# One visit of small TensorE tiles per slot beside the first batch's MLP, in a fused attention and MLP kernel

## The chip, the cores and the metric

The kernel runs on one core of one Trainium2 chip. The metric is the device time of one execution in microseconds (us). The kernel before takes 1423.95 us, the median of 7 runs (1421.37 to 1427.73).

## What is computed

Attention with normed queries and keys, then an MLP on the attention's output, in float32 (the two weight matrices arrive as float64):

```python
q_n, k_n = rmsnorm(q, g_q), rmsnorm(k, g_k)          # q, k, v: batch 8, heads 12, seq 448, head 64
attn = softmax(q_n @ k_n.T / sqrt(64))
x = (attn @ v), heads side by side: (3584, 768)
h = x @ w_in                                          # w_in (768, 2048)
out = (h - tanh(h)) @ w_out                           # w_out (2048, 768)
```

## The kernel before, in words

**Steps and slots.** The attention is cut into 48 steps s = 0 to 47, one for each batch and pair of heads, six (NP) for a batch. The program is written as a hand-made order (manual schedule): each engine executes its queue in the order in which the Python code issues instructions. One *slot* s issues the attention of step s, and preparations for steps s+1 to s+4. Slots -3 to 5 are `first_slot` (L879): attention only, no MLP. Slots 6 to 11 are `early_slot` (L913): the attention of the second batch beside the MLP of the first. Slots 12 to 47 are `slot` (L941): the attention of a batch beside the MLP of the batch before it.

**The MLP as a stream.** `mlp()` (L847) is a generator that yields after each matmul. `run(ns)` (L858) takes matmuls from it until so many nanoseconds of TensorE time, by a fixed price of each matmul, are used up. `gap_ns(s)` (L870) is a twelfth of the half of the MLP that runs beside three slots. So a slot's share of the MLP is four gaps in all, and the calls of `run` say between which pieces of attention the MLP stands. For the first batch the slots 6 to 8 run beside `hidden(0)` (L690, x times w_in as 4 sets of 7 products, L669) and the slots 9 to 11 beside `project_first` (L807, L834, 96 matmuls of 448 columns).

**The attention of one step** has these parts on TensorE, all of them with tiles smaller than the array:
- `scores(s, c)` (L486): for the key chunk c = 0, 1, 2, one matmul per head of 448 columns (L499), and for the rest of the keys (c = KF = 3) four of 224 columns. Each head's scores go to one PSUM bank, and ScalarE turns the bank into probabilities with an exponential (L504).
- `totals(s, dn)` (L557): the sum of the probabilities by a product with ones (L572) into one bank `dn`, then a reciprocal on VectorE (L577) that reads the bank. For s up to 9 the product runs over all chunks (16 matmuls). From s = 10 on VectorE has added the chunks before (`add` L513, `add_last` L524), and 4 matmuls are left. From s = 13 on (FOLDED) the sum takes another way, and `totals` is not called.
- `last_values` (L531, L539, 8 matmuls) and `values` (L544, L551, 24 matmuls): probabilities times v, into two banks `av`.
- `divide` (L607): VectorE multiplies the `av` banks by the reciprocals (L613) into xT, the MLP's input. For the last three pairs of a batch GpSimd makes differences of xT (L628 to L631).

Not small: `turn` (L410), eight transposes on the whole array (L415, L419), copied out by ScalarE (L417, L423).

**Banks.** PSUM has eight banks: three `mm` for the MLP and five `sc` for the attention, each set handed out in turn (`bank_of`, L198). A matmul that gets a bank waits until its reader of five allocations ago is done.

**The weights.** Beside the first slots and the first batch's MLP the kernel also turns the float64 weights into float32, in 32 pieces (`weight`, L290): a transfer into one of three `w_raw` buffers (L265, L269), two ScalarE passes (L71, L72), three VectorE passes (L78, L79, L82), and one GpSimd pass (L90), after which the buffer is free for the transfer three pieces on. Sets of w_in get sums and differences on VectorE (L324) and are stored for later batches (`keep_weights`, L329, seven transfers L332). The MLP's products call `weight` by a list of due times (`due`, L637), and `project_first` calls it with every sixth matmul. All of these stand in the same queues as the attention's exponentials, reciprocals and divisions.

**Norms.** `squares` (L393, ScalarE L123, L124) then `norm` (L396: VectorE L133, L134, GpSimd's power L135) then `norm_q` (L401: VectorE L404) prepare step s+3.

Of the kernel before, what the change touches and what calls it, by code (L numbers as in the profile page):

```python
# [137 lines left out]
def bounded_path(tc, ctx, q, k, v, moe_w_in, moe_w_out, out, g_col, ident, ones, half_ones, neg_half, early):  # L138
# [22 lines left out]
    NP = H // 2  # L161
# [13 lines left out]
    KF, KR = S // P, S % P  # L175
# [32 lines left out]
    def load(s, names):  # L208
        b, hp = steps[s]
        for name in names:  # L210
            src = {"q": q, "k": k, "v": v}[name]
            if s == 0 and name != "v":
                t = early[name]
            else:
                shape = [CP, 2, NCH, D] if name == "q" else [P, NCH, 2, D] if name == "k" else [P, 2, NCH, D]
                t = nat.tile(shape, F32, name=f"{name}_nat", bufs=3 if name == "v" else 2)
                fetch(nc, name, t, src[b, 2 * hp : 2 * hp + 2], by_blocks(s))
            loaded[name, s] = t
# [174 lines left out]
    def squares(s):  # L393
        squares_of(nc, early["sq"], early["n"], loaded["q", s], loaded["k", s])
# [15 lines left out]
    def turn(s, tk, tq):  # L410

        rr, n = normed.pop(s), early["n"]
        kn = loaded.pop(("k", s))
        for c in range(NCH):
            nc.tensor.transpose(tk[:, c * P : (c + 1) * P], kn[:, c].rearrange("p h d -> p (h d)"), ident)  # L415
        kT = qkp.tile([P, S], F32, name="kT")
        nc.scalar.mul(kT, tk[:, :S], g_col)  # L417
        for c in range(NCH):
            nc.tensor.transpose(  # L419
                tq[:, c * CP : (c + 1) * CP], n[:, c].rearrange("p h d -> p (h d)"), ident[:CP, :CP]  # L420
            )
        qT = qkp.tile([P, S], F32, name="qT")
        nc.scalar.copy(out=qT, in_=tq[:, :S])  # L423
        turned[s] = rr, kT, qT
# [5 lines left out]
    def by_blocks(s):  # L430
        return has(s) and steps[s][0] >= FIRST
# [51 lines left out]
    def sc_bank():  # L483
        return bank_of("sc")

    def scores(s, c):  # L486

        rr, kT, qT = turned[s]
        halves, keys, n = (1, P, S) if c < KF else (2, KR, HS)
        name, bufs = ("p", 2) if c < 2 else ("p_full", 1) if c < KF else ("p_last", 2)  # L490
        if c == 1:
            p = probs[s, 1] = probs[s, 0]
        else:
            p = probs[s, c] = pp.tile([P, 2, 2 if c < 2 else 1, n], F32, name=name, bufs=bufs)
        tiles = [sc_bank() for _ in range(2)]
        for i in range(halves):
            for h in range(2):
                r = slice(h * D, (h + 1) * D)
                nc.tensor.matmul(  # L499
                    tiles[h][i * keys : (i + 1) * keys, :n], lhsT=kT[r, c * P : c * P + keys],  # L500
                    rhs=qT[r, i * n : (i + 1) * n], start=True, stop=True,
                )
        for h in range(2):
            nc.scalar.activation(  # L504
                p[:, h, c if c < 2 else 0, :], tiles[h][:, :n], AF.Exp,
                scale=1.0 if rr is None else rr[:, 0, 2 * c + h : 2 * c + h + 1],
            )

    def full(s):

        return probs[s, 0][:, :, 0], probs[s, 1][:, :, 1], probs[s, 2][:, :, 0]
# [19 lines left out]
    def last_values(s, av):  # L531

        v_nat, p = loaded["v", s], probs[s, KF]
        for n in range(2):
            keys = slice(n * KR, (n + 1) * KR)
            for m in range(2):
                for h in range(2):
                    r = (2 * m + h) * BL
                    nc.tensor.matmul(  # L539
                        av[n][r : r + BL, :HS], lhsT=v_nat[keys, h, KF, m * BL : (m + 1) * BL],  # L540
                        rhs=p[keys, h, 0], start=True, stop=False,
                    )

    def values(s, av):  # L544
        v_nat, p = loaded.pop(("v", s)), full(s)
        for n in range(2):
            for c in range(KF):
                for m in range(2):
                    for h in range(2):
                        r = (2 * m + h) * BL  # L550
                        nc.tensor.matmul(  # L551
                            av[n][r : r + BL, :HS], lhsT=v_nat[:, h, c, m * BL : (m + 1) * BL],
                            rhs=p[c][:, h, n * HS : (n + 1) * HS], start=False, stop=(c == KF - 1),
                        )
        return av

    def totals(s, dn):  # L557

        parts = [t[:, h, n * HS : (n + 1) * HS] for t in sums.get(s, ()) for n in range(2) for h in range(2)]
        parts = [(parts, [ones[:, :BL]] * 2)] if parts else []  # L560
        if not sums.pop(s):
            for p in full(s):
                parts.append(
                    ([p[:, h, n * HS : (n + 1) * HS] for n in range(2) for h in range(2)], [ones[:, :BL]] * 2)
                )
            last = probs[s, KF]
            parts.append(([last[:, h, 0] for _ in range(2) for h in range(2)], [half_ones[:, n] for n in range(2)]))
        for i, (moving, by) in enumerate(parts):
            for n in range(2):
                for h in range(2):  # L570
                    r = (2 * n + h) * BL
                    nc.tensor.matmul(  # L572
                        dn[r : r + BL, :HS], lhsT=by[n], rhs=moving[2 * n + h],
                        start=(i == 0), stop=(i == len(parts) - 1),
                    )
        rs = whole[s] = sp.tile([P, HS], F32, name="rs")
        nc.vector.reciprocal(rs, dn[:, :HS])  # L577
# [29 lines left out]
    def divide(s, av):  # L607
        b, hp = steps[s]
        rs = whole.pop(s)
        x = xT[b, hp] = xp.tile([P, S], F32, name="xT")  # L610
        for n in range(2):
            for m in range(2):
                nc.vector.tensor_tensor(  # L613
                    out=x[m * D : (m + 1) * D, n * HS : (n + 1) * HS],
                    in0=av[n][m * D : (m + 1) * D, :HS],
                    in1=rs[:, n * HS : (n + 1) * HS] if s >= FOLDED else rs[n * D : (n + 1) * D], op=ALU.mult,
                )
        for c in range(NCH):
            del probs[s, c]
        if hp < HC:  # L620
            return
        c = hp - HC
        if c == 0:
            tt[b] = tp.tile([P, 3, HC, HS], F32, name="tt", bufs=1)
        eng = nc.vector if b == 0 and c == HC - 1 else nc.gpsimd
        x11, x12, x21, x22 = (xT[b, r][:, n : n + HS] for r in (c, hp) for n in (0, HS))
        t1, t2, t4 = (tt[b][:, i, c] for i in range(3))
        eng.tensor_tensor(out=t1, in0=x12, in1=x11, op=ALU.subtract)  # L628
        eng.tensor_tensor(out=t2, in0=x22, in1=t1, op=ALU.subtract)  # L629
        eng.tensor_tensor(out=x12, in0=x22, in1=x12, op=ALU.subtract)  # L630
        eng.tensor_tensor(out=t4, in0=x21, in1=t2, op=ALU.subtract)  # L631
# [226 lines left out]
    def run(ns):  # L858

        spent[1] += ns  # L860
        while spent[0] + 1.0 < spent[1]:
            took = next(stream, None)
            if took is None:
                return
            spent[0] += took
# [4 lines left out]
    def gap_ns(s):  # L870

        if s < 2 * NP:
            return H_NS / 12 if s % NP < 3 else 4 * S / ENGINE_NS * CD * CF / 12
        return (H_NS + O_NS) / (4 * NP)

    def has(s):
        return 0 <= s < NS
# [32 lines left out]
        weight(EARLY * (s + 3) // (NP + 2))  # L910
        combine(2)

    def early_slot(s):  # L913
        gap = gap_ns(s)
        totals(s, sc_bank())
        if has(s + 1):
            scores(s + 1, 0)
            scores(s + 1, 1)
        if has(s + 2):
            load(s + 2, "v")  # L920
        run(gap)
        if has(s + 2):
            turn(s + 2, sc_bank(), sc_bank())
        if has(s + 3):
            squares(s + 3)
        if has(s + 4):
            load(s + 4, "qk")
        run(gap)
        if has(s + 1):
            scores(s + 1, KF)  # L930
        av = [sc_bank() for _ in range(2)]
        last_values(s, av)
        divide(s, values(s, av))
        if has(s + 1):
            scores(s + 1, 2)
        for work, n in ((add, 1), (add_last, 1), (norm, 3), (norm_q, 3)):
            run(gap / 2)
            if has(s + n):
                work(s + n)

    def slot(s):  # L941

        gap = gap_ns(s)
# [59 lines left out]
    for s in range(-3, NP):  # L1003
        first_slot(s)
    for s in range(NP, NS):
        (early_slot if s < 2 * NP else slot)(s)
    run(1e9)


# [343 lines left out]
```

## Time and profile before

| what | value |
|---|---|
| median of 7 runs | 1423.95 us |
| the profiled execution, time | 1428.92 us |
| its span in the profile | 1427.1 us |
| busy share of the span: TensorE (PE), its weight loads (PEld) | 97%, 82% |
| VectorE (DVE), ScalarE (ACT), GpSimd (POOL) | 65%, 33%, 37% |
| mean granted TensorE clock | 0.988 |
| start of slots 6, 7, 8 (first matmul of `totals`) | 86.94, 118.28, 148.50 us |
| start of slots 9, 10, 11 | 189.24, 226.53, 262.83 us |
| start of slot 12 | 294.78 us |

The profile is of one execution. "Busy" is the time in which an engine has an instruction under way; idle time stands with what ended it. The clock granted to TensorE is a share of full speed. A float32 matmul has two records, so 16 matmuls are "x32". The chain of waits is followed back from the last instruction. The table by stage gives, for each stretch of time, the busy time of each engine, the granted clock, the busy share of the DMA engines and the rate.

### The profile page before, as it was taken

The page shows a single profiled execution, that of the slowest core. Times are in us where ns is not written, and L with a number is a line of the kernel's source. Part 1 is how long each engine was busy: PE and PEld are TensorE (multiplying, and loading weights), DVE is VectorE, ACT ScalarE, POOL GpSimd, SP SyncE. Part 2 cuts the span into 40 slices and gives each one's busy share as a digit, 9 for nine tenths or more (in the row PEclk, how much of TensorE's full clock was granted, in tenths as well). Part 3 has the DMA queues.
Part 4 walks back from the last instruction along what each step waited for, and adds up shares of the span by engine and source line. Part 5 has one row for each costly group of instructions (what it writes and reads, how often), then busy time and mean ns, then how long its engine had stood idle before and what let it go on. Part 6 is the DMA issues. An engine that isn't in the chain of part 4 may idle for free.

```text
span 1427.1 us, 25566 instructions
## 1 busy us (share of the span) xinstructions
PE 1388.4 (97%) x9752; PEld 1165.4 (82%) x9752; DVE 928.3 (65%) x1571; ACT 467.2 (33%) x1070; POOL 524.2 (37%) x348
## 2 busy tenths in 40 slices
PE   6999899999999999999999999999999999999997
PEld 3568664478899799888989888987998888899997
DVE  3899878867655677557866577655775578632311
ACT  5765445223422333232332234223332333301100
POOL 4565545314521336214543145312362145401310
PEclk9999899999999999999999999999999999999999
DMA  8669788764565655665656666666556656365563
GB/s 185 157 187 240 234 245 211 216 193 154 158 172 153 169 165 179 170 169 157 182 151 180 169 159 176 174 157 169 158 175 174 172 159 179 123 184 169 193 191 89
DMA packets 355255, 249.72 MB, mean 175 GB/s; under 512 B 266484, under 2 KB 297396, under 8 KB 355124
## 3 DMA queue, kind: packets, MB, share of 16 engines
q1 hardware_dynamic: 355120, 248.00, 62.7%
q8 instruction: 79, 1.29, 0.4%
q14 instruction: 52, 0.43, 0.1%
q10 hardware_dynamic: 4, 0.00, 0.0%
HBM read 214.50 MB, written 33.42 MB: 174 GB/s over the span
## 4 chain that ended last, share of the span: by engine, by line
PE 87%; DVE 6%; DMA 2%; SPq 2%; ACT 2%; issue 1%; POOL 0%; ACTq 0%; DVEq 0%
PE mm L669 63%; PE sc L499 9%; PE sc L551 7%; PE mm L834 5%; PE sc L539 2%; DMA w_raw<-in_moe_w_out_dram 1%; DVE w_out L82 1%; SPq L265 1%; ACT sum_g L592 1%; DMA k_nat<-in_k_dram 1%; DMA gT<-in_moe_w_in_dram 0%; SPq L118 0%; DVE rs L577 0%; DVE rows L529 0%; DVE sum_T L586 0%
## 5 line engine op out<-in xcount | busy, mean ns | idle before, releaser
L669 PE MATMUL mm<-xT,w_f 128*128 128x224 f32 x1392 | 275.6, 354 | 0.0
L669 PEld LDWEIGHTS mm<-xT,w_f 128*128 128x128 f32 x1392 | 262.1, 190 | 9.1 <-issue 7.2
L669 PE MATMUL mm<-gT,w_f 128*128 128x224 f32 x1344 | 263.0, 354 | 0.0
L669 PEld LDWEIGHTS mm<-gT,w_f 128*128 128x128 f32 x1344 | 252.8, 190 | 11.4 <-issue 6.5
L457 POOL TENSOR_TENSOR rr_mine<-rr_mine,neg_half 128x28 f32<-128x28 f32 x30 | 145.1, 4837 | 251.8 <-DVE rr_mine L456 251.8
L669 PE MATMUL mm<-tt,w_f 128*128 128x224 f32 x1044 | 209.4, 354 | 5.4 <-DVE gT L706 5.4
L669 PEld LDWEIGHTS mm<-tt,w_f 128*128 128x128 f32 x1044 | 196.5, 190 | 11.4 <-DVE gT L706 7.5
L669 PE MATMUL mm<-tg,w_f 128*128 128x224 f32 x1008 | 197.7, 352 | 0.0
L706 POOL TENSOR_TENSOR gT<-s,th 128x448 f32<-128x448 f32 x96 | 115.8, 1216 | 212.7 <-ACT th L705 211.7
L669 PEld LDWEIGHTS mm<-tg,w_f 128*128 128x128 f32 x1008 | 190.6, 190 | 0.0
L499 PE MATMUL sc<-qT,kT 64*128 64x448 f32 (+1 forms) x960 | 168.3, 499 | 12.6 <-ACT p_last L504 9.3
L499 PEld LDWEIGHTS sc<-qT,kT 64*128 64x128 f32 (+1 forms) x960 | 70.3, 167 | 85.2 <-issue 59.7
L592 ACT COPY sum_g<-sum 32x14 f32<-32x14 f32 x280 | 56.3, 201 | 225.3 <-DVE sum L588 219.5
L613 DVE TENSOR_TENSOR xT<-sc,rs_T 64x224 f32<-64x224 f32 x140 | 54.4, 389 | 68.3 <-PE sc L551 66.3
L629 POOL TENSOR_TENSOR tt<-xT,tt 128x224 f32<-128x224 f32 x23 | 17.1, 744 | 221.9 <-DVE xT L613 221.8
L504 ACT ACTIVATE p<-sc 128x448 f32<-128x448 f32 x120 | 55.5, 548 | 97.8 <-PE sc L499 97.8
L135 POOL TENSOR_TENSOR rr<-rr,neg_half 112x8 f32<-112x8 f32 (+1 forms) x36 | 59.8, 1682 | 63.3 <-DVE rr L134 63.2
L705 ACT ACTIVATE th<-s 128x448 f32<-128x448 f32 x96 | 55.0, 578 | 85.4 <-DVE s L731 37.6
L551 PE MATMUL sc<-p,v_nat 128*32 128x224 f32 x1344 | 79.9, 355 | 0.0
L834 PE MATMUL mm<-gT,w_out 128*128 128x448 f32 x192 | 77.4, 561 | 0.0
L521 DVE TENSOR_TENSOR rows<-p 128x896 f32<-128x896 f32 x38 | 42.4, 1115 | 41.7 <-ACT p L504 41.7
L834 PEld LDWEIGHTS mm<-gT,w_out 128*128 128x128 f32 x192 | 37.0, 197 | 38.2 <-issue 36.7
(144 smaller groups left out, 1753.2 us busy)
## 6 DMA issues: line engine op xcount, KB each, us to landing
w_f<-w_in SPq DMA_DIRECT2D x196, 384.0 KB, 3.1
w_f<-w_out SPq DMA_DIRECT2D x147, 512.0 KB, 3.8
w_raw<-in_moe_w_out_dram SPq DMA_DIRECT2D x16, 768.0 KB, 5.1
out_dram<-th SPq DMA_DIRECT2D x192, 56.0 KB, 1.9
w_in<-w_out SPq DMA_DIRECT2D x21, 384.0 KB, 6.0
qk_nat<-in_q_dram SPq DMA_DIRECT2D x120, 56.0 KB, 2.3
qk_nat<-in_k_dram SPq DMA_DIRECT2D x120, 56.0 KB, 2.3
gT<-in_moe_w_in_dram SPq DMA_DIRECT2D x32, 192.0 KB, 3.9
```

Source lines behind the costliest of these rows:

```text
L135: nc.gpsimd.tensor_tensor(out=r, in0=r, in1=neg_half[:rows], op=ALU.pow)
L457: nc.gpsimd.tensor_tensor(out=mine, in0=mine, in1=neg_half[:, :1].to_broadcast([P, 2 * NJ]), op=ALU.pow)
L499: nc.tensor.matmul(tiles[h][i * keys : (i + 1) * keys, :n], lhsT=kT[r, c * P : c * P + keys], rhs=qT[r, i * n : (i + 1) * n], start=True, ...
L504: nc.scalar.activation(p[:, h, c if c < 2 else 0, :], tiles[h][:, :n], AF.Exp, scale=1.0 if rr is None else rr[:, 0, 2 * c + h : 2 * c + h ...
L521: nc.vector.tensor_tensor(out=t, in0=p[0], in1=p[1], op=ALU.add)
L551: nc.tensor.matmul(av[n][r : r + BL, :HS], lhsT=v_nat[:, h, c, m * BL : (m + 1) * BL], rhs=p[c][:, h, n * HS : (n + 1) * HS], start=False, ...
L592: nc.scalar.copy(out=acc[h * BL : (h + 1) * BL, g], in_=part[g * BL : (g + 1) * BL, h * NJ : (h + 1) * NJ])
L613: nc.vector.tensor_tensor(out=x[m * D : (m + 1) * D, n * HS : (n + 1) * HS], in0=av[n][m * D : (m + 1) * D, :HS], in1=rs[:, n * HS : (n + ...
L669: nc.tensor.matmul(bank[:, f * HS : (f + 1) * HS], lhsT=w[:, c * width + f, :], rhs=moving[p](c), start=(first and f == 0 and c == 0), sto ...
L705: nc.scalar.activation(th, h, AF.Tanh, bias=0.0, scale=1.0)
L706: eng.tensor_tensor(out=g[:, rows, cols], in0=h, in1=th, op=ALU.subtract)
L834: nc.tensor.matmul(bank[:, :S], lhsT=w_out_row(f, n // HC)[:, n % HC * P : (n % HC + 1) * P], rhs=g[:, f, :], start=(f == 0), stop=(f == C ...
```

## The change

`early_slot` is removed, and the slots 6 to 11 use `slot`:

```diff
-    def early_slot(s):
-        gap = gap_ns(s)
-        totals(s, sc_bank())
-        if has(s + 1):
-            scores(s + 1, 0)
-            scores(s + 1, 1)
-        if has(s + 2):
-            load(s + 2, "v")
-        run(gap)
-        if has(s + 2):
-            turn(s + 2, sc_bank(), sc_bank())
-        if has(s + 3):
-            squares(s + 3)
-        if has(s + 4):
-            load(s + 4, "qk")
-        run(gap)
-        if has(s + 1):
-            scores(s + 1, KF)
-        av = [sc_bank() for _ in range(2)]
-        last_values(s, av)
-        divide(s, values(s, av))
-        if has(s + 1):
-            scores(s + 1, 2)
-        for work, n in ((add, 1), (add_last, 1), (norm, 3), (norm_q, 3)):
-            run(gap / 2)
-            if has(s + n):
-                work(s + n)
...
     for s in range(NP, NS):
-        (early_slot if s < 2 * NP else slot)(s)
+        slot(s)
```

What `slot` issues for these six slots (the parts for later batches, which test `blocks` and `folded`, issue nothing here):

```python
    def slot(s):
        gap = gap_ns(s)
        scores(s + 1, KF)
        dn = sc_bank()
        av = [sc_bank() for _ in range(2)]
        last_values(s, av)
        totals(s, dn)
        divide(s, values(s, av))
        for c in range(KF):
            scores(s + 1, c)
        load(s + 2, "v")
        run(gap / 2)
        add(s + 1)
        run(gap / 2)
        turn(s + 2, sc_bank(), sc_bank())
        squares(s + 3)
        load(s + 4, "qk")
        run(gap / 2)
        add_last(s + 1)
        run(gap / 2)
        norm(s + 3)
        run(gap)
        norm_q(s + 3)
        run(gap)
```

So the two visits of small tiles, before at the slot's start and in its middle, become one at its start, with the sums' product between the last chunk's values and the other values. The same matmuls, exponentials, divisions and transfers are issued as before. `norm` stands after two gaps (before: three and a half), `norm_q` after three (before: four), `add` and `add_last` half a gap and one and a half gaps after the visit. Slots -3 to 5 and 12 to 47 are unchanged.

## Prediction, on record before the run

> **What bounds the kernel now.** I read the table by stage first, cut at the starts of slots. Its columns: stretch, length, busy time of TensorE, weight loads, VectorE, ScalarE, GpSimd, then granted clock, DMA share, GB/s. Slots 7 to 11 of before:
>
> ```profile
> 118.28:148.50 30.22, 30.22 (x238) 25.55 (x237) 28.06 (x38) 16.77 (x28) 19.16 (x13) 1.00 0.94 283
> 148.50:189.24 40.74, 34.81 (x237) 28.32 (x236) 33.31 (x39) 20.05 (x31) 18.60 (x10) 0.87 0.69 217
> 189.24:226.53 37.29, 34.98 (x189) 17.31 (x188) 32.23 (x35) 16.87 (x27) 23.19 (x15) 0.95 0.79 216
> 226.53:262.83 36.30, 34.65 (x165) 16.67 (x164) 32.40 (x46) 12.86 (x22) 19.45 (x13) 0.95 0.82 218
> 262.83:294.78 31.95, 31.95 (x165) 15.78 (x165) 22.82 (x37) 7.29 (x14) 8.13 (x7) 1.00 0.84 236
> ```
>
> Slots 7 and 11 are TensorE from end to end. Slot 8 has slot 7's matmuls and takes 10.5 us longer; slots 9 and 10 are 5.3 and 4.35 us longer than slot 11 (of the 5.3, 1.1 is the longer sums' product). VectorE is busy 28 to 33 us in each, so it has little slack. TensorE's waits between 86.94 and 294.78 us:
>
> ```profile
> PE sc L499 <- ACT p_last L504: 7.6, 2, 5.9
> PE sc L415 <- DVE rs L577: 2.3, 1, 2.3
> PE mm L669 <- DVE s L725: 0.3, 1, 0.3
> ```
>
> So 10.2 us of idle. ScalarE's rows by time at the longest wait show why: the exponential stands behind a weight pass that waits for its transfer.
>
> ```profile
> 171.82 0.91 ACT L71 ACTIVATE w_out<-w_raw 128x768 f32<-128x768 f32 x1 [5.11 <-DMA w_raw<-in_moe_w_out_dram]
> 172.63 0.90 ACT L72 ACTIVATE w_raw<-w_raw 128x768 int32<-128x768 uint32 x1
> 173.43 0.77 ACT L504 ACTIVATE p_last<-sc,rr 128x224 f32<-128x224 f32 x2
> ```
>
> Idle time costs twice. The table by stage after the waits of 5.9, 2.3 and 1.65 us shows the clock at half:
>
> ```profile
> 174.00:176.00 2.00, 2.00 (x3) 0.71 (x4) 1.60 (x5) 0.91 (x3) 1.63 (x1) 0.50 0.86 226
> ...
> 203.00:205.00 2.00, 2.00 (x4) 1.01 (x3) 1.97 (x3) 2.00 (x5) 1.17 (x1) 0.50 1.11 347
> ...
> 250.00:252.00 2.00, 2.00 (x4) 0.95 (x3) 1.91 (x4) 0.00 (x0) 1.92 (x3) 0.50 0.59 91
> ```
>
> The prices by clock are 0.13 of 40.74 (5.3 us) in slot 8, 0.05 of 37.29 (1.9) in slot 9, 0.05 of 36.30 (1.8) in slot 10.
>
> [...] Here 1.65 us of idle sufficed. [...]
>
> **What the change removes.** Nothing is computed less. Slot 12 of before already runs the new order; its visit by rows of TensorE:
>
> ```profile
> 294.78 0.61 PE L499 MATMUL sc<-qT,kT 64*64 64x224 f32 x8
> 295.32 0.61 PE L539 MATMUL sc<-p_last,v_nat 64*32 64x224 f32 x16
> 295.86 0.59 PE L572 MATMUL sc<-rows,ones 128*32 128x224 f32 x8
> ...
> 298.15 0.56 PE L551 MATMUL sc<-p_full,v_nat 128*32 128x224 f32 x8
> 298.64 2.79 PE L499 MATMUL sc<-qT,kT 64*128 64x448 f32 x12
> ```
>
> By the chain of waits this visit is 0.54 + 0.54 + 0.52 + 2.27 + 2.72 = 6.59 us; slot 11's two visits are 0.52 + 1.71 and 0.54 + 0.54 + 2.41 + 0.95, together 6.67. The first run of MLP matmuls after a visit is 0.18 us longer than one after the transposes (5.49 against 5.31 for 28). So one visit less saves 0.08 + 0.18 = 0.26 us a slot, 1.5 us in six. That is the sure part, and all of it if nothing else moves.
>
> **What it adds: a wait within the visit.** Before, the banks of `totals` and `values` were wanted again half a slot later. Now five banks serve one visit: `scores(s+1, 1)` takes the bank of `totals`, so it waits for the reciprocal, and the first `values` bank, and `scores(s+1, 2)` the second, so they wait for `divide`. Behind the waiting score stands all of TensorE. The cover is `values` and chunk 0's scores, 2.27 + 0.95 = 3.2 us; slot 12's visit shows no wait there. But beside the weights VectorE is late. In before the reciprocal followed the end of its product by:
>
> - slot 7: 5.4 us (125.35 against 119.94), slot 8: 3.3, slot 9: 8.7 (199.58 against 190.9), slot 10: 5.6 (232.71 against 227.1), slot 11: 2.1.
>
> With the reciprocal's 1.55 us and up to 1.64 us of divisions after it, a visit would wait between nothing and 7 us. What shortens the lags: `norm_q` (1.0 us alone, up to 3.05 us while GpSimd's power is late) leaves its place right ahead of the reciprocal, and GpSimd gets a gap instead of half a gap for the power. For each visit nothing and the old lag are the two ends.
>
> [...]
>
> **The walk, slot by slot**, with durations of before. An undisturbed slot is slot 7 less 0.26, 29.95 us (slots 6 to 8), or slot 11 less 0.15, 31.8 us (slots 10, 11). The last scores chunks begin 5.9 us after the start (slots 6 to 9) or 4.8.
>
> - *Slot 6* starts at 86.94. `last_values` waits for the exponentials that end at 88.26; `totals` ends at 90.25; the reciprocal, behind the weights' passes as before, ends at 94.96, the divisions at 96.6, the visit at 97.4. With four gaps and `turn` (22.2) slot 7 starts at 119.6: +1.4 us against before.
> - *Slot 7*: a wait of 0 to 3.0 us for VectorE; I take 2, nearer the old lag, since VectorE is full there. Slot 8 starts at 151.6: +3.1.
> - *Slot 8*: the reciprocal (153.45 to 155 before) is in time for 157.5. The wait of 5.9 us can't occur in its place: no exponential stands in mid-slot behind the weight pass, and the MLP's three banks let TensorE go on for a product or two (2.3 us each) while a tanh is late. Slot 9 starts at 181.5: -7.7.
> - *Slot 9*: the weights are late now. The exponentials of the visit stand behind the pass of the piece that was treated at 193.13 before. Its transfer waited for a chain that had itself stood still with TensorE (ScalarE's tanh waited for TensorE until 182.60), so it comes earlier, but seven stores fill the DMA engines until about 184 (400 GB/s). I put the exponentials at 191.3, between 186.5 (no wait) and 195.2 (as before). TensorE wants them at 186.5 and waits 4.8 us, pays some 2.5 us of clock, and ends the visit at 197. The 2.3 us wait of `turn` for the reciprocal, with its 1.9 us, goes: the reciprocal is over by then. With 25.2 us of MLP and `turn` slot 10 starts at 222.2: -4.3.
> - *Slot 10*: 31.8 plus 1 us of waiting for VectorE, in place of 36.30. Slot 11 starts at 255.0: -7.8.
> - *Slot 11*: 31.8 against 31.95. Slot 12 starts at 286.8: -8.0.
>
> The walk is too kind to VectorE: I took a weight piece's three passes at 2.06 us, while their means here, beside a busy GpSimd, are 852 + 895 + 1042 ns = 2.79 us. Four such passes lie on the chain that ends in slot 9's exponentials and slot 7's reciprocal: 3 us back. The forecast is **-5 us**.
>
> The profiled execution took 1428.92 us, 0.35% over the median of the runs, for a span of 1427.1. Made against it the sum gives 1423.9; a difference of -5 on the median of 1423.95 gives **1419.0 us**. About 0.2% (2.8 us) is what a measurement of this kernel can tell from no change.
>
> **Rivals.**
> 1. *VectorE's lag becomes the bound of the visits (slower).* Place: chunk 1's scores in slots 6 to 10. With the old lags the visits would wait 2.2, 3.9, 1.8, 7.2 and 4.1 us, 19 us, and five clock prices of 1.7 us, 8.5: 27.7 us. Against this go the 1.5 us saved and, of the old excess (9.5, 4.2 and 4.35), between 4.2 and 18. That gives +8 to +22; with half the lags gone +3. It decides once the reciprocal begins more than 1.7 us (3.2 less 1.55) after the product. For it: VectorE's busy 28 to 33 us. Against: the lags are work of VectorE that time spent waiting lets it finish. At its middle 1433 us; chance 0.28.
> 2. *The wait only moves (no change).* The pieces' chain (transfer, ScalarE, VectorE, GpSimd, three buffers) sets the pace, and slot 9's exponentials come at 195.2 as before. The visit then ends near 201, where before stands at 192.6 plus 4.4 for the visit still owed plus 4.2 for the wait of `turn`, 201.2. Slot 10's gain goes to a weight wait of its own. 1423; chance 0.17.
> 3. *No visit meets a late weight pass.* The excess of slots 8 to 10 goes but for a few us: -10 to -16, 1411; chance 0.05.
>
> That the program would not do what the diff says is excluded: built, TensorE's queue has the new order in all six slots.
>
> **How the numbers follow.** The forecast's own case (-3 to -10 us) has 0.50. Faster by over 0.2%: 0.50 + 0.05 = 0.55; within: 0.17; slower: 0.28. The range 1409 to 1433 takes in the forecast, no change, most of case 3 and half of rival 1; about 0.17 is left out.
>
> **What would show it.** Right: slot 8 near 30 us in place of 40.7; the largest wait at `scores` chunk 0 of slot 9, for an exponential (L504); no wait of L415 for L577; slots 6 and 7 1 to 3 us longer. Wrong: waits of L499 for L577 or L613 over 2 us in several slots (rival 1), or slot 9 starting early and ending late by the same amount (rival 2). From slot 12 on nothing should differ but the offset.

## The result, and the profile after

The changed kernel takes **1429.40 us** (median of 18 runs), the kernel before 1423.42 (46 runs): ratio 1.0040, 95% interval 1.0031 to 1.0049. It is slower by some 6 us; forecast was 1419.0, 5 us faster. A second set of its runs (e15 below) came out at 1.0023 (1.0008 to 1.0037): slower again, by some 3 us. The profiled execution of the changed kernel took 1430.26 us for a span of 1428.5.

The table by stage of the changed kernel, slots 6 to 11 (stretch, length, busy time of TensorE, weight loads, VectorE, ScalarE, GpSimd, then granted clock, DMA share, GB/s):

```profile
84.49:119.78 35.29, 33.68 (x239) 26.79 (x237) 32.44 (x46) 18.68 (x31) 16.12 (x10) 0.95 0.62 164
119.78:153.41 33.63, 32.48 (x238) 26.81 (x237) 26.96 (x38) 17.04 (x29) 18.26 (x12) 0.95 0.70 194
153.41:191.98 38.57, 32.78 (x238) 27.25 (x237) 35.75 (x43) 17.79 (x29) 22.20 (x12) 0.96 0.75 251
191.98:229.53 37.55, 34.38 (x190) 18.98 (x189) 29.49 (x36) 18.16 (x28) 22.68 (x15) 0.95 0.76 217
229.53:264.79 35.26, 34.39 (x166) 16.82 (x165) 31.75 (x41) 13.92 (x22) 20.13 (x12) 0.95 0.80 223
264.79:296.43 31.64, 31.64 (x166) 16.27 (x165) 22.17 (x37) 7.21 (x14) 6.44 (x5) 1.00 0.82 225
```

Against before (31.34, 30.22, 40.74, 37.29, 36.30, 31.95 us) the slots are longer by 3.95 and 3.41, shorter by 2.17, longer by 0.26, shorter by 1.04 and 0.31: together 211.94 against 207.84 us, +4.1. From slot 12 to the end nothing differs (1132.07 against 1132.32 us). The spans differ by 1.4 only, because slot 6 began at 86.94 us in before's profiled execution and at 84.49 in this one; in the runs e4, e5, e11 and e12 below, whose code is before's up to there, it began at 84.2 to 84.9. So the medians are the measure.

TensorE's waits in the changed kernel between 84.49 and 296.43 us (total, times, longest):

```profile
PE mm L669 <- DVE s L727: 4.3, 1, 4.3
PE sc L499 <- ACT p_last L504: 3.2, 1, 3.2
PE sc L499 <- DVE rs L577: 3.2, 3, 1.1
PE mm L669 <- DVE s L725: 1.5, 1, 1.5
...
```

This is 12.6 us where before had 10.2. The exponential's 5.9 us in slot 8 and the turn's 2.3 us in slot 9 are gone. In their place stand 4.3 and 1.5 us of MLP products in slot 8 that wait for VectorE's additions (L725, L727), three waits of scores for the reciprocal, and 3.2 us at the start of slot 9.

**The reciprocal in the visit.** VectorE by time in slot 7 of the changed kernel:

```profile
123.60 0.96 DVE L82 SCALAR_TENSOR_TENSOR w_f<-w_raw,w_f 128x768 int32<-128x768 int32 x1
124.47 0.95 DVE L324 TENSOR_TENSOR w_f<-w_f 128x768 f32<-128x768 f32 x1
125.34 1.55 DVE L577 RECIPROCAL rs<-sc 128x224 f32<-128x224 f32 x1
127.00 1.63 DVE L613 TENSOR_TENSOR xT<-sc,rs 64x224 f32<-64x224 f32 x4
```

TensorE in the same visit:

```profile
124.78 1.02 PE L499 MATMUL sc<-qT,kT 64*128 64x448 f32 x4
126.94 3.75 PE L499 MATMUL sc<-qT,kT 64*128 64x448 f32 x8 [1.15 <-DVE rs L577]
```

A weight piece's passes, of which the last (L82) is shown, and a sum (L324) stand ahead of the reciprocal. It ends at 126.89, and at 126.94 chunk 1's scores start, 1.15 us late.

**The wait that the list of waits doesn't have.** Those four score matmuls (x8: two records each) take 3.75 us. In slot 7 of before four of them ran so:

```profile
119.94 1.77 PE L499 MATMUL sc<-qT,kT 64*128 64x448 f32 x8
```

Part of the difference is the clock (below). The rest shows in the run e3, whose slot 7 is in the new form and ran at full clock:

```profile
124.55 1.02 PE L499 MATMUL sc<-qT,kT 64*128 64x448 f32 x4
126.71 2.76 PE L499 MATMUL sc<-qT,kT 64*128 64x448 f32 x8 [1.13 <-DVE rs L577]
```

The view of line L499 alone, in e3 between 124.5 and 129.8 us, counts weight loads with matmuls: idle time before them, and what ended it (us, times):

```profile
its engine sat idle before it (us, times) until:
  DVE rs L577: 3.0, 2
  DVE xT L613: 1.1, 2
  issue: 0.4, 1
```

Two heads' scores use half of the array's rows each (64) and run side by side: in chunk 0 their first matmuls start at 124.55 and 124.56. In chunk 1 the first head's bank comes from the reciprocal, the second's from the first half of the divisions. The heads start at 126.71 and 127.60 us, one after the other, and each takes some 0.9 us, the time in which both would run. Price: 2.76 less 1.77, **1.0 us** a visit. TensorE counts as busy in it, since the records overlap: in slot 7 of the changed kernel the first head's last record runs from 127.43 to 127.96, and the second head's first starts at 127.84. Slots 6 (e3: 2.79) and 10 (e13: 2.78) show the same, slot 8 a row of x12 with 3.41 us in place of slot 11's 2.76.

Before pays this price too, in its two waits for an exponential: the second head's scores of chunk 2 come after the wait, alone. Slot 10 of before, and slot 11, where nothing waits:

```profile
245.30 1.02 PE L499 MATMUL sc<-qT,kT 64*128 64x448 f32 x2
247.97 1.02 PE L499 MATMUL sc<-qT,kT 64*128 64x448 f32 x2 [1.65 <-ACT p_last L504]
...
281.60 1.02 PE L499 MATMUL sc<-qT,kT 64*128 64x448 f32 x4
```

After the wait the second head takes TensorE for 0.94 us more (the next matmul starts at 248.91). In slot 8 it takes 1.79 us, at half clock. So each of these two waits cost some 0.95 us beyond its length, the clock apart.

**The MLP in slot 8.** TensorE's two late products of the changed kernel:

```profile
178.71 2.54 PE L669 MATMUL mm<-xT,w_out 128*128 128x224 f32 x12 [1.48 <-DVE s L725]
185.55 4.04 PE L669 MATMUL mm<-xT,w_out 128*128 128x224 f32 x12 [4.31 <-DVE s L727]
```

VectorE meanwhile:

```profile
173.50 2.21 DVE L78 TENSOR_SCALAR w_out<-w_out 128x768 f32<-128x768 f32 x1
...
178.04 0.62 DVE L725 TENSOR_TENSOR s<-mm,s 128x448 f32<-128x448 f32 x1
178.57 1.94 DVE L78 TENSOR_SCALAR w_out<-w_out 128x768 f32<-128x768 f32 x1
180.54 0.56 DVE L79 TENSOR_SCALAR w_out<-w_out 128x768 int32<-128x768 int32 x1
181.14 0.96 DVE L82 SCALAR_TENSOR_TENSOR w_out<-w_raw,w_out 128x768 int32<-128x768 int32 x1
182.02 0.68 DVE L133 TENSOR_REDUCE rr<-n 112x8 f32<-112x512 f32 x1
182.73 1.45 DVE L134 TENSOR_SCALAR rr<-rr 112x8 f32<-112x8 f32 x1
184.10 0.67 DVE L133 TENSOR_REDUCE rr<-sq 128x8 f32<-128x512 f32 x1
...
184.88 0.62 DVE L727 TENSOR_TENSOR s<-mm,s 128x448 f32<-128x448 f32 x1
```

VectorE has no gap of more than 0.1 us here. Each addition that frees a bank of the MLP stands behind a weight piece, the second also behind `norm` (L133, L134), which now comes earlier. Before, VectorE caught up during TensorE's stand of 5.9 us in mid-slot, and then waited for TensorE itself:

```profile
179.09 0.62 DVE L727 TENSOR_TENSOR s<-mm,s 128x448 f32<-128x448 f32 x1 [3.39 <-PE mm L669]
```

**Slot 9.** ScalarE at the start of slot 9 of the changed kernel:

```profile
195.18 0.94 ACT L71 ACTIVATE w_out<-w_raw 128x768 f32<-128x768 f32 x1 [8.05 <-DMA w_raw<-in_moe_w_out_dram]
...
197.66 0.92 ACT L71 ACTIVATE w_out<-w_raw 128x768 f32<-128x768 f32 x1 [0.23 <-DMA w_raw<-in_moe_w_out_dram]
...
199.74 0.75 ACT L504 ACTIVATE p_last<-sc,rr 128x224 f32<-128x224 f32 x2
```

As foreseen, the visit's exponential stands behind weight passes that wait for a transfer; it came at 199.74, not at 191.3 (the wait was shorter than the walk's because slot 9 itself began late).

**The clock.** The table by stage of the changed kernel, cut into half microseconds, at the edges of what the clock lost:

```profile
94.00:94.50 0.50, 0.50 (x4) 0.26 (x4) 0.47 (x2) 0.16 (x1) 0.00 (x0) 0.75 1.04 215
97.50:98.00 0.50, 0.50 (x4) 0.47 (x3) 0.50 (x1) 0.50 (x1) 0.50 (x1) 0.83 0.00 0
128.00:128.50 0.50, 0.50 (x2) 0.13 (x2) 0.47 (x2) 0.50 (x1) 0.00 (x0) 0.89 0.58 147
```

A mean of 0.75 between 1.00 and 0.50 puts the fall in the middle of its half microsecond, at 94.25; 0.83 puts the return at 97.67: 3.4 us at half clock. The third row (0.89) puts the next fall at 128.39; the others, read in the same way, are at 186.41, 200.07 and 237.61. So there are five such stretches between slots 6 and 12, at most 1.7 us lost in each. Before has five as well (three of them in a row, from 171.07 to 181.31). What is lost I take as half of the time that TensorE is busy in them (before's second head above took 1.79 us at half clock, 0.94 at full): it is busy 16.92 us there in the changed kernel and 14.22 in before, where the wait of 5.9 us takes up part of the first. So the clock costs 8.5 us, before 7.1.

**The sum** in this pair of profiles: idle +2.4; the heads that no longer run side by side +3.65 (1.0 in slots 6, 7 and 10, 0.65 in slot 8) less before's 1.9; clock +1.4; one visit less in six slots -1.5. Together +4.05, where +4.1 was measured.

### The profile page after: what moved, and what is told of

Same layout as the page of the kernel before. It is cut to its first block, busy times and chain, and to the rows that moved or that the text cites. A ratio compares the mean times of both kernels' runs of the same rounds, so it can differ in the third digit from the quotient of the medians.

```text
span 1428.5 us, 25550 instructions
## 1 busy us (share of the span) xinstructions
PE 1388.1 (97%) x9752; PEld 1169.1 (82%) x9752; DVE 928.0 (65%) x1571; ACT 467.4 (33%) x1070; POOL 527.3 (37%) x348
## 3 DMA queue, kind: packets, MB, share of 16 engines
q8 instruction: 79, 1.29, 0.4%
## 4 chain that ended last, share of the span: by engine, by line
PE 85%; DVE 7%; DMA 3%; ACT 2%; issue 1%; SPq 1%; POOL 0%; ACTq 0%; DVEq 0%; POOLq 0%
PE mm L669 61%; PE sc L499 10%; PE sc L551 6%; PE mm L834 4%; PE sc L539 1%; DMA gT<-in_moe_w_in_dram 1%; DMA w_raw<-in_moe_w_out_dram 1%; DMA q_nat<-in_q_dram 1%; PE mm L551 1%; DVE rs L577 1%; DVE w_out L78 1%; ACT sum_g L592 1%; DVE w_out L79 1%; DVE rows L529 0%; DVE sum_T L586 0%
## 5 line engine op out<-in xcount | busy, mean ns | idle before, releaser
L669 PE MATMUL mm<-xT,w_f 128*128 128x224 f32 x1392 | 275.5, 353 | 0.0
L669 PEld LDWEIGHTS mm<-xT,w_f 128*128 128x128 f32 x1392 | 262.2, 190 | 8.5 <-issue 6.5
L669 PE MATMUL mm<-gT,w_f 128*128 128x224 f32 x1344 | 263.0, 354 | 0.0
L669 PEld LDWEIGHTS mm<-gT,w_f 128*128 128x128 f32 x1344 | 252.8, 190 | 11.4 <-issue 5.9
L669 PE MATMUL mm<-tt,w_f 128*128 128x224 f32 x1044 | 209.4, 354 | 5.4 <-DVE gT L706 5.4
L669 PEld LDWEIGHTS mm<-tt,w_f 128*128 128x128 f32 x1044 | 196.5, 190 | 11.4 <-DVE gT L706 7.5
L669 PE MATMUL mm<-tg,w_f 128*128 128x224 f32 x1008 | 197.7, 352 | 0.0
L669 PEld LDWEIGHTS mm<-tg,w_f 128*128 128x128 f32 x1008 | 190.6, 190 | 0.0
L499 PE MATMUL sc<-qT,kT 64*128 64x448 f32 (+1 forms) x960 | 172.6, 508 | 10.6 <-ACT p_last L504 4.5
L499 PEld LDWEIGHTS sc<-qT,kT 64*128 64x128 f32 (+1 forms) x960 | 74.2, 170 | 85.2 <-issue 56.3
L135 POOL TENSOR_TENSOR rr<-rr,neg_half 112x8 f32<-112x8 f32 (+1 forms) x36 | 60.2, 1693 | 70.8 <-DVE rr L134 68.6
```

Source lines behind the costliest of these rows:

```text
L135: nc.gpsimd.tensor_tensor(out=r, in0=r, in1=neg_half[:rows], op=ALU.pow)
L499: nc.tensor.matmul(tiles[h][i * keys : (i + 1) * keys, :n], lhsT=kT[r, c * P : c * P + keys], rhs=qT[r, i * n : (i + 1) * n], start=True, ...
L669: nc.tensor.matmul(bank[:, f * HS : (f + 1) * HS], lhsT=w[:, c * width + f, :], rhs=moving[p](c), start=(first and f == 0 and c == 0), sto ...
```

## The experiments

Theory A puts the loss into the visits, where TensorE waits for VectorE; its rival B puts it elsewhere, so that freeing the visit would not bring it back. "Idle" is the sum of TensorE's listed waits from slot 6 up to slot 12 in the run's profile, "half" the number of 3.41 us stretches at half clock there. Each run's ratio is to the runs of before made beside it (medians 1423.17 us for e1 to e4, 1424.98 for e5 to e8, 1424.18 for e9 to e12, 1423.67 for e13 to e15), so ratios compare better than medians.

| kernel | median us | ratio to before (95%) | idle us | half |
|---|---|---|---|---|
| before | 1423.42 | 1 | 10.2 | 5 |
| after | 1429.40 | 1.0040 (1.0031 to 1.0049) | 12.6 | 5 |
| e15 after again | 1427.95 | 1.0023 (1.0008 to 1.0037) | 12.4 | 5 |
| e1 scores later | 1422.23 | 0.9983 (0.9971 to 0.9996) | 8.9 | 4 |
| e2 scores twice | 1424.98 | 1.0007 (0.9994 to 1.0020) | 10.0 | 2 |
| e3 slots 6 to 8 | 1426.06 | 1.0013 (1.0001 to 1.0026) | 10.2 | 3 |
| e4 slots 9 to 11 | 1427.39 | 1.0024 (1.0013 to 1.0035) | 12.4 | 4 |
| e5 preparations only | 1419.55 | 0.9961 (0.9948 to 0.9975) | 6.8 | 2 |
| e6 visit only | 1442.04 | 1.0125 (1.0106 to 1.0143) | 19.9 | 7 |
| e7 before, light VectorE | 1415.44 | 0.9938 (0.9923 to 0.9953) | 7.8 | 2 |
| e8 after, light VectorE | 1419.67 | 0.9963 (0.9950 to 0.9977) | 9.2 | 3 |
| e9 before, no late loads | 1415.30 | 0.9931 (0.9912 to 0.9949) | 4.4 | 1 |
| e10 after, no late loads | 1423.99 | 0.9997 (0.9984 to 1.0009) | 8.1 | 2 |
| e11 later last scores | 1414.37 | 0.9929 (0.9911 to 0.9946) | 4.1 | 0 |
| e12 late norm, slot 6 | 1419.55 | 0.9967 (0.9953 to 0.9982) | 5.3 | 2 |
| e13 late norm, slot 8 | 1428.88 | 1.0030 (1.0015 to 1.0045) | 13.6 | 3 |
| e14 e1 with e13 | 1422.55 | 0.9989 (0.9977 to 1.0001) | 11.5 | 3 |

**e1: chunks 1 and 2 of the scores half a gap later, in slots 6 to 11** (against after)

```diff
+        split = s < 2 * NP
         if has(s + 1):
-            for c in range(KF):
+            for c in range(1 if split else KF):
                 scores(s + 1, c)
...
         run(gap / 2)
+        if split:
+            scores(s + 1, 1)
+            scores(s + 1, 2)
```

> The changed kernel, but in slots 6 to 11 the scores of chunks 1 and 2 stand half a gap later, after the first MLP matmuls, so that TensorE doesn't meet the reciprocal's bank in the visit. Theory A (the loss is TensorE's wait of 0.9 to 1.15 us for the reciprocal in slots 6, 7 and 10, and the clock that halves after it, 2 to 2.7 us more each): these waits go, 3 x 3.4 us less 6 x 0.26 us for the extra change between MLP and small tiles, so about 8 us faster than the changed kernel, ratio to before about 0.998 (0.996 to 1.000). Theory B (the loss lies in the moved norms, sums and loads, which stay where the change put them): no gain over the changed kernel, ratio 1.004 to 1.006.

TensorE's rows of the same scores in slot 7 of e1:

```profile
124.71 1.02 PE L499 MATMUL sc<-qT,kT 64*128 64x448 f32 x4
128.51 1.77 PE L499 MATMUL sc<-qT,kT 64*128 64x448 f32 x8
```

No wait for the reciprocal is left in any slot, every row of 8 takes 1.77 us, and slot 7 is 30.08 us long (the walk's undisturbed slot: 29.95). e1 is 0.6% faster than after, some 8 us: theory A's number came, and B's (no gain) did not. The matmuls and banks are those of after; only the time between freeing and use is longer.

**e2: chunk 0's scores multiplied twice in slots 6, 7 and 10** (against after)

```diff
...
-                scores(s + 1, c)
+                scores(s + 1, c, 2 if c == 0 and s in (6, 7, 10) else 1)
```

> The changed kernel, but in slots 6, 7 and 10 chunk 0's scores are multiplied twice into the same banks (the same values again): 0.95 us more work for TensorE just ahead of each of the three waits, nothing moved on any other engine. Theory A with the clock as the larger part of the price: the waits shrink from 1.1 to 0.2 us, the clock stays full, and each visit ends some 2 us earlier: 5 to 7 us faster than the changed kernel, ratio to before 0.999 to 1.001. Theory A without the clock (a wait costs its length): the added work takes the wait's place, no difference, 1.004. Theory B: the work is added on top, 1.005 or more.

With six matmuls more (x12) it is 0.3% faster than after. Its waits for the reciprocal were 1.99 us in slot 6 and 0.40 in slot 7, not 0.2 as expected, and no stretch at half clock followed either. The rows of 8 still take 2.79 and 2.76 us: the repeated matmuls fill the wait for the first bank, not the lag between the two heads' banks. So the lag is a cost by itself, apart from the wait and from the clock.

**e3 and e4: the change in slots 6 to 8 alone (e3), or in 9 to 11 alone (e4)**, both against before

```diff
-        (early_slot if s < 2 * NP else slot)(s)
+        (early_slot if NP + 3 <= s < 2 * NP else slot)(s)
```

> The change in slots 6 to 8 alone; slots 9 to 11 as in the kernel before. By the slots' lengths in the two profiles (after less before: +3.95, +3.4, -2.2 us for slots 6, 7, 8 and +0.3, -1.0, -0.3 for 9, 10, 11) it costs 5 us: ratio 1.0036, and more if slot 9 in its old form meets the late weights worse. If the loss were spread over all six slots (Theory B, what is moved is moved in each): about 1.002.

```diff
-        (early_slot if s < 2 * NP else slot)(s)
+        (early_slot if s < NP + 3 else slot)(s)
```

> The change in slots 9 to 11 alone; slots 6 to 8 as in the kernel before. By the same table it gains 1 us: ratio 0.9993; with the wait in slot 10 still there (3.4 us) and the old wait of the transposes in slot 9 gone (4.2 us). Theory B (spread over all six): about 1.002.

The halves add up: 0.13% and 0.24% to the whole's 0.40%. Both missed: e3 was to cost 0.36%, and I had not expected the second half to lose. What came is nearer theory B's 1.002 for each half: the loss is spread over both. In e4's profile slot 8 (old form) keeps the wait of 5.94 us, and slot 9's visit then waits 1.42 us for an exponential and 4.07 for the reciprocal; the turn's wait that goes was 2.3.

**e5: before's two visits, after's earlier `norm` and `norm_q`; e6: after's visit, before's later preparations** (both against before)

```diff
         run(gap)
+        norm(s + 3)
         if has(s + 1):
             scores(s + 1, KF)
...
-        for work, n in ((add, 1), (add_last, 1), (norm, 3), (norm_q, 3)):
-            run(gap / 2)
-            if has(s + n):
-                work(s + n)
+        run(gap / 2)
+        add(s + 1)
+        run(gap / 2)
+        add_last(s + 1)
+        norm_q(s + 3)
+        run(gap)
```

> The kernel before with its two visits per slot, but norms, norm_q and sums in slots 6 to 11 at the places where the change put them (norm after two gaps, norm_q after three, sums half a gap earlier in the order). Theory A (the loss is TensorE's wait for the reciprocal's bank in the one visit, so here nothing is lost): ratio to before 0.998 to 1.001. Theory B (the moved preparations cost the time): 1.003 or more.

```diff
-        totals(s, sc_bank())
-        if has(s + 1):
-            scores(s + 1, 0)
-            scores(s + 1, 1)
...
+        scores(s + 1, KF)
+        dn = sc_bank()
+        av = [sc_bank() for _ in range(2)]
+        last_values(s, av)
+        totals(s, dn)
+        divide(s, values(s, av))
+        for c in range(KF):
+            scores(s + 1, c)
...
```

> The other half alone: one visit per slot as in the change, but turn, norms, norm_q and sums in slots 6 to 11 at their places of the kernel before (norm after three and a half gaps, norm_q right at the slot's end, ahead of the reciprocal in VectorE's queue). Theory A: at least the change's loss, more where norm_q now stands between TensorE's product and the reciprocal: 1.004 to 1.010, with longer waits of L499 for L577. Theory B: about 1.000.

TensorE's waits in e5:

```profile
PE sc L499 <- ACT p_last L504: 4.9, 2, 4.1
PE mm L669 <- DVE s L735: 1.3, 1, 1.3
...
```

TensorE's waits in e6:

```profile
PE sc L499 <- DVE rs L577: 8.9, 4, 4.1
PE sc L499 <- ACT p_last L504: 7.9, 1, 7.9
...
```

This takes the change apart, but for one piece: the sums (`add`, `add_last`) stand in both runs where before has them, though e5's expectation has them moved. The one visit alone costs 1.25%, some 18 us: four waits for the reciprocal (1.92, 1.29, 4.14 and 1.53 us), one of 7.93 for the exponential, and seven stretches at half clock; that is more than I had expected. The earlier norms alone *gain* 0.39%, which I had not expected: with them no transposes wait for the reciprocal, and three of five stretches at half clock go. In the new order the earlier preparations (there with the sums) give back 0.85 of the 1.25%. I had treated the two as one edit.

**e7 and e8: VectorE lighter**, in before and in after (without L79, one of a weight piece's three passes)

```diff
-    nc.vector.tensor_scalar(
-        out=bits, in0=bits, scalar1=4, scalar2=1, op0=ALU.logical_shift_left, op1=ALU.logical_shift_right
-    )
```

> The kernel before without one of VectorE's three passes over the weights (L79, the shift of the bits, is left out, so the weights are wrong): 24 passes of 0.56 to 0.9 us less on VectorE beside slots 6 to 10. It is the yardstick of the next run. Both theories: some 3 to 10 us faster than before (0.993 to 0.998), by shorter waits in slots 8 to 10.

> The changed kernel without the same pass. Theory A (the reciprocal comes late because VectorE's queue is full of weight passes): the reciprocal is in time, the waits of L499 for L577 in slots 6, 7, 10 are gone or under 0.5 us, and the change now costs nothing against the light kernel before: between 3 us less and 1 us more than that run. Theory B: it still costs about 6 us against that run.

e7 is 0.62% and e8 0.37% under before. The new order is still 4.2 us behind the old, where theory A had it at -3 to +1. Slot 7's wait for the reciprocal went, but 1.18 us stayed in slot 6 and 0.86 in slot 10, and 3.7 us at the MLP in slot 8. So it isn't VectorE's load alone; I take the rest to be the order of its queue.

**e9 and e10: no late transfers** (before and after without the fetches of pieces 19 to 31)

```diff
...
-        else:
+        elif n < CF + 3:
             raw = wp.tile([P, 2 * DM], I32, name="w_raw", bufs=3)
+            late_raw[n] = raw
+        else:
+            raws[n] = late_raw[CF + (n - CF) % 3].rearrange("p (n w) -> p n w", w=2)
+            return
```

> The kernel before, but the weight pieces 19 to 31 aren't fetched: they get the old data of the three buffers (the result is wrong), with all passes on ScalarE, VectorE and GpSimd as before. Theory A says of slots 8 to 10: what is late there in both kernels is the chain of the pieces, and the change only moves the wait (before: TensorE waits 5.9 us in slot 8's second visit; changed: 1.5 and 4.3 us in slot 8's MLP and 3.2 in slot 9's visit). Without the transfers the 5.9 and 1.65 us waits should shrink to under 1 us: 8 to 14 us faster than before (0.990 to 0.994). If the transfers aren't the cause but VectorE's passes: under 4 us.

> The changed kernel without the same transfers. Theory A: its waits in slot 8's MLP and slot 9's visit shrink too, the waits for the reciprocal in slots 6 and 7 (1.1 us and clock) stay: 8 to 12 us faster than the changed kernel, and still 3 to 7 us slower than the run without late loads of the kernel before. If the change's loss came from the late transfers in slot 8 and 9: no difference left between the two, or a gain of 1.5 us for the one visit.

TensorE's waits in e10 (its lines are 4 higher, so L731 is L727, L581 is L577 and L729 is L725):

```profile
PE mm L673 <- DVE s L731: 4.2, 1, 4.2
PE sc L503 <- DVE rs L581: 1.9, 3, 1.1
...
PE mm L673 <- DVE s L729: 1.5, 1, 1.5
```

Slot 9's 3.17 us for the exponential are gone (0.48 for the reciprocal stand there): that wait was the transfers'. Slot 8's 1.5 and 4.2 us stay within 0.1: those aren't, where I had expected them to shrink. The old order gains 0.69% by it, as expected, the new 0.43%, less than expected, so the new is 8.7 us behind: its loss isn't owed to late transfers.

**e13 and e14: slot 8's `norm` and `norm_q` back to their later places**, in after and in e1

```diff
-        if ahead:
+        if ahead and s != 8:
             norm(s + 3)
...
         run(gap / 2)
+        if s == 8:
+            norm(s + 3)
...
```

> The changed kernel, but in slot 8 norm and norm_q at their places of the kernel before. If the 4.3 us wait for the addition L727 is largely the early norm ahead of it (2.9 us on VectorE in the changed kernel's profile), it falls to about 1.5 us, and slot 8 gets 3 to 4 us shorter; part comes back in slot 9, whose reciprocal then stands behind norm_q: 0 to 4 us faster than the changed kernel, ratio to before 1.001 to 1.004. If the weight passes alone are the cause, the wait stays at 4 us, and the ratio is 1.004 or more.

> The run with the scores of chunks 1 and 2 half a gap later (0.9983), with slot 8's norm and norm_q late as in the run above. The reciprocal isn't waited for here, so what slot 8 gains isn't lost in slot 9: 2 to 4 us faster than that run, ratio to before 0.9955 to 0.997. If the norm isn't the cause: 0.998.

TensorE's rows of e13 at the end of slot 8 and in slot 9:

```profile
184.38 2.54 PE L669 MATMUL mm<-xT,w_out 128*128 128x224 f32 x12 [1.44 <-DVE s L727]
189.12 0.61 PE L499 MATMUL sc<-qT,kT 64*64 64x224 f32 x8
201.38 5.14 PE L499 MATMUL sc<-qT,kT 64*128 64x448 f32 x12 [7.19 <-ACT p_last L504]
```

The wait for L727 falls from 4.31 to 1.44 us, so `norm` was two thirds of it, and slot 8 takes 34.0 us in place of 38.57. All of it comes back one slot later (42.42 us in place of 37.55): the exponential's wait grows from 3.17 to 7.19, and chunk 0's scores start at 201.38 (after: 200.22). e14 shows it once more (1.44 us, then 7.5) and gains nothing on e1, where I had expected 0.2 to 0.3%. So once TensorE no longer stands still in slot 8, the pieces' chain sets when slot 9's visit can go on. e13's time lay in its range, but I had the loss come back by the reciprocal, not by the exponential, and e14 missed. Both say the same: the gain of slot 8 was not to be had by either order.

**e11 and e12, from e5:** e11 also puts chunk 2's scores half a gap later in slots 8 and 10; e12 puts slot 6's `norm` back

```diff
-        if has(s + 1):
+        later = s in (8, 10)
+        if not later:
             scores(s + 1, 2)
         run(gap / 2)
+        if later:
+            scores(s + 1, 2)
```

> The run with the preparations alone (two visits, norms and sums early, ratio 0.996), and in slots 8 and 10 the scores of chunk 2 half a gap later, where TensorE waited 4.1 and 0.8 us for an exponential behind a late weight pass. If that wait is for the exponential alone, 2 to 4 us faster than that run (0.9935 to 0.995). If the MLP's own additions behind VectorE's weight passes take its place, as in the changed kernel's slot 8, no gain (0.996 or more).

> The run with the preparations alone, but with slot 6's norm and norm_q at their places of the kernel before. In that run TensorE waited 1.35 us in slot 6 for an addition (L735) that stands behind the early norm. If the norm ahead of it is the cause, the wait goes: 1 to 3 us faster (0.994 to 0.9955). Else no difference.

e11 is the fastest, 0.7% under before. Its waits:

```profile
PE mm L669 <- DVE s L735: 1.3, 1, 1.3
PE sc L499 <- ACT p_last L504: 1.2, 1, 1.2
...
```

The 5.9 us of slot 8 became 1.2, and no stretch ran at half clock: the last scores moved out of the second visit, the opposite of the change, is what gains. e12 missed: slot 6's wait of 1.35 us went, slot 8's grew from 4.10 to 4.72, the time stayed.

**e15: after again**

> The changed kernel once more. The ratio to before should be 1.004 again. In its first profile the clock fell to half after waits of 1.14, 1.15 and 0.87 us in slots 6, 7 and 10; in runs with the same program up to slot 8 it didn't, after 1.66 and 1.13 us. If the halving depends on where a short wait lies in time, this profile shows the same waits with another pattern of full and half clock; if the wait's length decides, it shows the same pattern.

The ratio was 1.0023, not 1.004; the intervals of the two sets (1.0031 to 1.0049, 1.0008 to 1.0037) overlap. Up to the start of slot 9 the slots' starts repeat within 0.4 us, and the waits in them within 0.1. The wait in slot 10 was 0.64 us in place of 0.87, and the clock didn't fall there; the wait at slot 9's start was 3.3, and it fell for two stretches in place of one. In slots 6 to 8 the pattern is the same, but so, nearly, is the place of the waits in time (the clock falls at 94.39 and 128.52 us, in the first profile at 94.25 and 128.39), so the question asked of this run stays open.

## Why the prediction was wrong

By slots, the walk had lengths of 32.7, 32.0, 29.9, 40.7, 32.8 and 31.8 us; measured were 35.29, 33.63, 38.57, 37.55, 35.26 and 31.64. The sum is 12.1 us too short, 3 of which the "3 us back" took in.

- **Slot 8, the step that failed** ("The wait of 5.9 us can't occur in its place ... the MLP's three banks let TensorE go on for a product or two"): -10.8 us on before was forecast, -2.2 came. That the exponential's wait goes was right. That three banks would cover was wrong: it was argued for a late tanh, while VectorE's additions also free these banks, and they stood behind two weight pieces and `norm` (1.48 and 4.31 us). I had looked at one reader of the banks only. And e13 and e14 show that what is saved here waits in slot 9.
- **The visits of slots 6, 7 and 10**: 2.6, 1.6 and 2.5 us longer than the walk. The waits for the reciprocal were smaller than I took (1.15 us in slot 7 against 2; 0.87 in slot 10 against 1). The terms that were missing are the two heads out of step (1.0 us each) and the clock after each wait (0.05 x 33.63 = 1.7 us in slot 7). Slot 7 closes with them: 29.95 + 1.15 + 1.0 + 1.7 = 33.8 against 33.63. The prediction has 1.65 us of idle cost clock, but the walk leaves that price out of slots 6, 7 and 10.
- **Slot 9**: right in place and kind, too high in size: 40.7 against 37.55, with a wait of 3.17 us in place of 4.8. The turn's wait for the reciprocal is gone, as foreseen.
- **Slots 10 and 11**: -3.5 and -0.15 forecast, -1.04 and -0.31 measured; slot 10's miss is the visit's.
- **A reading of before that was off**: the prediction has the clock take 5.3 us in slot 8, by the slot's whole length. TensorE stood still for 2.8 us of the 10.24 at half clock, so the clock took 3.7, and the second head alone took 0.95. So slot 8's excess of 10.5 us over slot 7 is 5.93 + 0.95 + 3.7 = 10.6, and slot 10's 4.35 over slot 11 are 1.65 + 0.95 + 1.7 = 4.3. The heads out of step, which the walk lacks, already stood in before's rows.
- **Saved by one visit less**: e3's slot 7 (32.07 us) less its wait of 1.13 and the 1.0 of the heads is 29.94 against 30.22, so 0.28 where 0.26 was taken.
- **Rival 1** named the mechanism (chunk 1's scores wait for VectorE) and the sign. Its sizes were wrong: waits of 0.87 to 1.15 us, not 2.2 to 7.2, because the earlier norms shorten the lags; without them (e6) they are 1.3 to 4.1 us and the loss 18 us, within its +8 to +22. **Rival 2** holds where slot 8 passes into slot 9: the pieces' chain keeps the pace there.
- The signs named ahead: slot 8 near 30 us did not come; slots 6 and 7 grew by 3.95 and 3.41, not 1 to 3; no wait of L499 for L577 exceeded 2 us, and yet they cost more than they show.

What stays open: in these profiles the slots differ by 4.1 us and the medians by 6; single executions of one kernel lie up to 6 to 8 us apart (1426.07 to 1432.48, and 1420.63 to 1428.39), and with one profile each I can't say more.

## What to carry to other kernels

Merging two visits that share a ring of PSUM banks shortens the time from the freeing of a bank to its next use; look at what stands ahead of *every* reader of the banks in its engine's queue, and split such an edit into its order and its moved preparations before judging it (here +1.25% and -0.39%, and +0.40% together). Where two half-array matmuls run side by side, look at both banks: here a lag of 0.9 us between them cost 0.95 to 1.0 us, about the length of one head's scores, without appearing among the waits. A wait removed from a chain that another chain paces can come back where the two meet (in e13 slot 8's fell from 4.31 to 1.44 us, and slot 9's grew from 3.17 to 7.19), so ask what else is late there before booking it.

## What the runs showed of the hardware

**The clock fell on a grid of 3.41 us.** The five falls in the changed kernel's profile lie 34.14, 58.02, 13.66 and 37.54 us apart: 10, 17, 4 and 11 times 3.414. The stretches at half clock last 3.41 us or a multiple (94.25 to 97.67 us here; 171.07 to 181.31, three in a row, in before). I laid the idle time of TensorE over windows of this grid from 62 to 300 us, in all 17 profiles:

| idle in a window at full clock | windows | next one at half clock |
|---|---|---|
| 0.15 to 0.86 us | 56 | 0 |
| 0.87 to 1.78 us | 40 | 10 |
| 1.79 us and more | 38 | 38 |

The bounds are drawn where the outcomes part. In the middle class none of the 14 windows whose waits were at the MLP's whole-array products (L669) was followed by half clock, but 9 of the 20 at the scores and one of the 6 at the transposes were. No run was made to test why. So nearly the same wait may cost its length or 1.7 us more: 1.13 us in slot 7 of e3 cost no clock, 1.15 in the changed kernel did. What decides between the two isn't shown.

In the changed kernel three windows with a wait for the reciprocal were idle for 0.87 to 1.15 of their 3.41 us, and the clock was at half in the next one each time.

**VectorE's pass L78 was late beside GpSimd's L90.** In slot 8 of the changed kernel (the rows shown above) VectorE's L78 takes 2.21 us at 173.50 and 1.94 at 178.57; at 185.95, where GpSimd runs another operation (L135), it takes 0.55. GpSimd by time:

```profile
172.85 2.45 POOL L90 TENSOR_TENSOR w_out<-w_out,w_raw 128x768 int32<-128x768 int32 x1 [1.54 <-PE mm L669]
...
178.25 1.84 POOL L90 TENSOR_TENSOR w_out<-w_out,w_raw 128x768 int32<-128x768 int32 x1 [1.54 <-issue]
```

These end at 175.30 and 180.09; the two L78 that began beside them end at 175.71 and 180.51, 0.41 and 0.42 us later. So do two more that began inside an L90: 153.18 (1.88 us, end 0.42 us after it) and 189.14 (1.67 us, 0.42). A fifth, at 227.08 inside the L90 from 226.69 to 229.33, took 0.55 us; there the L79 after it took 2.08 (0.56 at 186.53) and ended 0.41 us after the L90. Not every operation was slow: L732, an addition that reads a bank of the MLP, took its usual 0.61 us at 166.81, inside the L90 from 165.62 to 168.07.
